# FNet plus MLP-Mixer block in one kernel: first matrix piece loaded from GpSimd, and a smaller idle tile

## The chip, the cores and the metric

The kernel runs on 1 core of one Trainium2 chip. The metric is the device time of one execution in microseconds; the time before is 865.86 us, the median of 3 runs (865.59 to 866.18).

## The reference

With x of 2048 rows and 640 columns (one batch), xn is x with each row brought to mean 0 and variance 1 (eps 1e-5), and the output is a sum of three terms:

```python
xn = layernorm(x)
a, b = xn @ Wd_re.T, xn @ Wd_im.T           # 640 x 640 matrices
fnet = Ws_re @ a - Ws_im @ b                # 2048 x 2048 matrices
h = layernorm(xn)
u = gelu(h.T @ w1 + b1)                     # w1: 2048 x 1728
mixer = (u @ w2 + b2).T                     # w2: 1728 x 2048
out = x + fnet + mixer
```

Everything is float32.

## The kernel before, in words

Each float32 matrix product is made of three TensorE matmuls over operands split into a high and a low part (high by high, high by low, low by high); a *piece* is 128 x 512 values of a matrix that was loaded from memory and is cut into such a pair, the high part by ScalarE (`high`, L143) and the low part by VectorE (`low`, L146). The work is a list of steps; each has a top (cut the high part), a bottom (cut the low part) and a run (its matmuls). The first stage multiplies columns of the sequence matrices, `dft_seq`, with the normalized rows of x (matmuls on L494 and L654); then come the hidden matrices, the two mixer products (`sup`, `sdown`, L154 to L157) and the sums with the output. Program order is the order on each engine, with no reordering (`manual_schedule`).

The start, which the change touches, is written out by hand as a table of words, `START` (L42 to L48). A letter names a function in `first_columns` (table on L556), the number its argument. `x0` to `x7` load 128 rows of x each (320 KB; x0 in two halves of 160 KB, L518; the others on L520). `b0` to `b7` load a piece of `dft_seq` each (256 KB, `load`, L482), and `W1-1-0` and its like load pieces for the next columns (L584). All these loads are issued on SyncE's queue (SP), in the order of the table. Then come the words of the computation: `M` and `A` are the row statistics (L218, L221), `R` the reciprocal root on ScalarE (`near`, L227), `D0` the first block of the high part of row block 0, columns 0 to 255 (`first_hi`, L381, VectorE), `T` and `B` the top and bottom of a step, `O` and `V` the exact factors, five small operations of GpSimd in a chain (L238, L243, L244, L245, L238), `N` and `H` the normalized rows and their high parts on ScalarE (L273) or VectorE (L552), `L` their low parts on VectorE (L146), and `P` a step's matmuls. `T0` cuts piece b0 in two halves: columns 0 to 255 by ScalarE (L143), 256 to 511 by VectorE (CAST, L193). The first real matmul needs both halves and `D0`. Its third pass (`P0-2`) needs the low part of row block 0, which comes at the end of the chain of exact factors.

Ahead of all that, VectorE sets a tile of ones and then a 128 x 512 bfloat16 tile of zeros, `idle` (L137), and TensorE runs ten matmuls of it with itself into a bank that is not read (L140, `WARM`); GpSimd sets `eps` (L133) and runs one operation on it (L135).

Of the kernel before, what the change touches and what calls it, by code (L numbers as in the profile page):

```python
# [10 lines left out]
BF16 = mybir.dt.bfloat16  # L11
AF = mybir.ActivationFunctionType
ALU = mybir.AluOpType

P = 128
# [10 lines left out]
CH = 512  # L26
NC = S // CH
H2 = D // 2
EPS = 1e-5
# [10 lines left out]


START = """  # L42
    x0 b0 W1-1-0 x1 b1 x2 W1-1-1 b2 W1-1-2 x3 b3 W1-1-3 x4 b4 x5 b5 x6 b6 x7 b7 W2-1-0 W2-1-1 W2-1-2 W2-1-3
    M0 A0 R0 D0 T0 O0 V0 H0 B0 T1 P0-0-1 B1 M1 A1 N0 R1 O1 V1 T2 H1 L0 P1-0-1 P0-2 P1-2 B2 M2 A2 T3 R2 O2 T4 V2 H2 B3 N1 P2-0-1 L1 P3-0-1 P2-2 P3-2
    M3 A3 R3 O3 V3 B4 N2 M4 A4 T5 R4 H3 V4 B5 L2 T6 N3 M5 A5 B6 P4-0-1 P5-0-1 P4-2 P5-2 T7 R5 V5 L3 N4 B7 H4 M6 A6 T8 P6-0-1 P6-2 R6 V6 M7 A7 B8 E0-0 E0-1 E0-2 N5 P7
    R7 V7 L4 T9 P8-0-1 P8-2 H5 B9 N6 T10 P9-0-1 L5 P9-2 H6 B10 N7 T11 P10-0-1 L6 P10-2 H7 B11 T12 P11-0-1 L7 P11-2
# [24 lines left out]
def fnet_plus_mixer(  # L71
# [30 lines left out]
    nc = tc.nc  # L102

    keep = ctx.enter_context(tc.tile_pool(name="keep", bufs=1))
# [7 lines left out]
    eps = keep.tile([P, 1], F32, name="eps")  # L112
    idea = keep.tile([P, 1], F32, name="idea")
# [15 lines left out]
    y_part = [[dram.tile([P, ND, CH], F32, name=f"y{m}{c}") for c in range(NC)] for m in range(2)]  # L129


    nc.vector.memset(one, 1.0)
    nc.gpsimd.memset(eps, EPS)  # L133
    nc.scalar.activation(one, one, AF.Abs_reciprocal_sqrt)
    nc.gpsimd.tensor_scalar(idea, eps, EPS, eps, op0=ALU.add, op1=ALU.mult)  # L135
    idle = keep.tile([P, CH], BF16, name="idle", tag="slab7")
    nc.vector.memset(idle, 0.0)  # L137
    psum = [acc.tile([P, CH], F32, name=f"psum{i}") for i in range(8)]
    for i in range(WARM):
        nc.tensor.matmul(psum[7], idle[:, :P], idle, start=True, stop=True)  # L140

    def high(hi, src):
        nc.scalar.activation(hi, src, AF.Copy)  # L143
# [31 lines left out]
    def cut_piece(source, n, tail=False, stacked=False, by_two=False):  # L175

        held = {}

        def of_tail():
            hi, src = (t.rearrange("p (q c) -> p q c", c=P) for t in (held["piece"][:, 0, :n], source()))
            return hi[:, :, :TAIL], hi[:, :, P - TAIL :], src[:, :, :TAIL]

        def top():
            cut_turn[0] = (cut_turn[0] + 1) % (AHEAD + 1)
            held["piece"] = keep.tile([P, 2, D], R32, name="piece", tag=f"cut{cut_turn[0]}")
            if tail:
                hi, _, src = of_tail()
                high(hi, src)  # L190
            elif by_two:
                high(held["piece"][:, 0, : n // 2], source()[:, : n // 2])
                nc.vector.tensor_copy(held["piece"][:, 0, n // 2 : n], source()[:, n // 2 :])  # L193
            else:
                high(held["piece"][:, 0, :n], source())

        def bottom():
            if tail:
                hi, lo, src = of_tail()
                low(lo, src, hi)  # L200
                return held["piece"][:, 0, :n], None
            hi, lo = (held["piece"][:, i, :n] for i in range(2))
            if stacked:
                last = slice(n - P, n)
                low(hi[TAIL:, last], source()[TAIL:, last], hi[TAIL:, last])
            whole = n - P if stacked else n
            low(lo[:, :whole], source()[:, :whole], hi[:, :whole])
            return hi, lo

        return top, bottom  # L210
# [12 lines left out]
    def root(var, q=None):  # L223

        if q is None:
            q = small.tile([P, NS], F32, name="q")[:, : var.shape[-1]]
        nc.scalar.activation(q, var, AF.Abs_reciprocal_sqrt, bias=eps)  # L227
        return var, q

    def inverse(to, var, q):  # L230

        r = small.tile([P, NS], F32, name="r")[:, : var.shape[-1]]
        nc.vector.scalar_tensor_tensor(r, var, EPS, q, op0=ALU.add, op1=ALU.mult)
        nc.vector.scalar_tensor_tensor(r, r, -0.5, q, op0=ALU.mult, op1=ALU.mult)
        nc.vector.scalar_tensor_tensor(to, r, 1.5, q, op0=ALU.add, op1=ALU.mult)
# [12 lines left out]
    def offset(to, ks):  # L248
        nc.vector.scalar_tensor_tensor(to[:, 1, ks], mv[:, ks, 0], -1.0, to[:, 0, ks], op0=ALU.mult, op1=ALU.mult)
# [56 lines left out]
    def fifth(a, which, i):  # L306
        return a[:, which, 7 * Q + i * P : 7 * Q + (i + 1) * P]
# [90 lines left out]
    def later_row(k):  # L398
        return later_pair(k % 4)[:, (k - 8) // 4, :]
# [58 lines left out]
    def c_tile():  # L458

        i = c_turn[0] = (c_turn[0] + 1) % 6  # L460
        return c_place[i // 3][:, i % 3, :]
# [9 lines left out]
    def first_columns():  # L471


        raw = pieces[0].rearrange("p a q c -> p (a q) c")
        banks = {0: psum[0], 1: psum[1], 2: psum[7]}
        vq = {}

        def place_of(i):
            return raw[:, (i + 4) % 8, :]

        def load(i):
            nc.sync.dma_start(place_of(i), dft_seq[0, i])  # L482

        def products(i):
            a, n = fixed[0][i % 4], i // 4

            def run(w, passes=()):
                blocks = [
                    (banks[e], *((a[:, k, n * Q + e * P : n * Q + (e + 1) * P]) for k in range(2))) for e in range(2)
                ] + [(banks[2], fifth(a, 0, n), fifth(a, 1, n))]  # L490
                for one in ([blocks] if passes else [[b] for b in blocks]):
                    for k in passes or range(3):
                        for to, hi, lo in one:
                            nc.tensor.matmul(  # L494
                                to, (hi, hi, lo)[k], w[k % 2], start=k == 0 and i == 0, stop=k == 2 and i % 4 == 3,
                                skip_group_check=True,
                            )
            return run

        def read(i, e):  # L500


            c = c_tile()
            nc.scalar.activation(c, banks[e], AF.Copy)
            if i == 0:
                to = ((1, 4),) if e == 2 else ((1, e), (0, 2 + e), (1, 2 + e))
            else:
                to = ((0, 4 if e == 2 else e),)
            for m, j in to:
                nc.sync.dma_start(y_part[m][0][:, j, :], c)  # L510

        raw_steps.extend(cut_piece(lambda i=i: place_of(i), CH, by_two=i == 0) + (products(i),) for i in range(8))


        def row(k):
            if k == 0:
                for i in range(2):
                    nc.sync.dma_start(x_in[0][:, i * H2 : (i + 1) * H2], x_rows[0][:, i * H2 : (i + 1) * H2])  # L518
            else:
                nc.sync.dma_start(x_in[k], x_rows[k])  # L520

        def begin_loads(i):
            for f in loads.pop(i, ()):
                f()

        def top(i):
            steps[i][0]()

        def bottom(i):
            ready[i] = steps[i][1]()  # L530

        def run(i, *passes):
            steps[i][2](ready[i], *([passes] if passes else []))
            if not passes or 2 in passes:
                del ready[i]

        def rooted(k, to=None, by=1):
            ks = slice(k, (to or k) + 1, by)
            vq[k] = root(mv[:, ks, 1], near[:, 0, ks])

        def inverted(k, to=None, by=1):
            inverse(norm[:, 0, slice(k, (to or k) + 1, by)], *vq[k])

        def factored(k, to=None, by=1):
            inverted(k, to, by)
            offset(norm, slice(k, (to or k) + 1, by))

        def whole_row(k):
            if k in BY_SCALAR:
                return normalize(k, x_in[k], norm)  # L550

            nc.vector.tensor_scalar(  # L552
                x_in[k], x_in[k], mv[:, k, 0:1], norm[:, 0, k : k + 1], op0=ALU.subtract, op1=ALU.mult
            )

        return {  # L556
            "x": row, "b": load, "q": begin_loads, "T": top, "B": bottom, "P": run,
            "M": lambda k: statistics(k, x_in[k] if k < 8 else later_row(k)), "A": aggregate,
            "R": rooted, "F": factored, "I": inverted, "O": lambda k: offset_beside(near, k), "V": factors_beside,
            "D": lambda k: first_hi(),  # L560
            "H": lambda k: first_rows(k, 0), "N": whole_row,
            "L": lambda k: first_rows(k, 1), "E": read,
            "X": lambda i: [f() for f in extras.pop(i)],
            "J": lambda q, j: (sums_left.remove((j, q)), first_sums[q][j]()),
            "W": lambda i, m, q: first_loads.pop((f"B{i}{m}", q))(),
        }
# [580 lines left out]
    start = first_columns()  # L1147
# [49 lines left out]
    gets_hid, _, rests_hid = zip(*(hidden_rows(q, ("x0", "v")[q % 2]) for q in range(3)))  # L1197
# [100 lines left out]
```

## Time and profile before

| | |
|---|---|
| time, median of 3 runs | 865.86 us (865.59 to 866.18) |
| profiled execution, its own time | 865.11 us |
| profiled execution, span from first to last instruction | 863.3 us |
| TensorE busy with matmuls | 858.4 us (99% of the span) |
| VectorE, ScalarE, GpSimd busy | 697.0, 529.2, 179.6 us |
| DMA, mean over the span | 185 GB/s |
| granted TensorE clock, mean | 1.000 |

The span lies 1.8 us below the execution's own time; what is outside it is not in the trace. A row of the chain of waits is a start, a duration and what ran, or which transfer was waited for; a row of the timeline adds the engine, line, operation, tiles and count, and in brackets how long the engine had been idle and what ended that. "SPq" is SyncE issuing transfers, "PEld" a weight load.

### The profile page before, as it was taken

To read this page: it belongs to the slowest core of one execution; us is meant where nothing else is said; L and a number is where in the kernel's file an instruction comes from. 1 tells how busy PE (TensorE), PEld (TensorE's weight loads), DVE (VectorE), ACT (ScalarE), POOL (GpSimd) and SP (SyncE) were. 2 spreads that over 40 slices of the span, in tenths; PEclk is the share of its full clock that TensorE was granted. 3 is DMA by queue.
4 is the path that set the end of the run, shared out by engine and by line. 5 is a ranking of instruction groups with operands and counts; after the bars stand their busy time and mean duration, and the time that the engine had idled before them with its cause. 6 is when DMAs were issued, how large, how long until landed. Compare 5 with 4: busy or idle time off the path is not lost.

```text
span 863.3 us, 13976 instructions
## 1 busy us (share of the span) xinstructions
PE 858.4 (99%) x4882; PEld 786.8 (91%) x4882; DVE 697.0 (81%) x1173; ACT 529.2 (61%) x987; POOL 179.6 (21%) x249
## 2 busy tenths in 40 slices
PE   9999999999999999999999999999999999999998
PEld 6888888888888888889999999999999999999998
DVE  7998868784757888877887788888678978897887
ACT  7766676755444555657565556676577856555654
POOL 5333222212120211122100101111321321101211
PEclk9999999999999999999999999999999999999999
DMA  8879594979593746779576766664678789766776
GB/s 316 287 217 324 127 301 125 253 188 296 145 261 63 200 96 140 175 130 206 114 180 169 158 144 184 195 180 154 149 175 186 160 226 237 184 140 132 155 168 148
DMA packets 93350, 159.44 MB, mean 185 GB/s; under 512 B 9408, under 2 KB 37824, under 8 KB 92928
## 3 DMA queue, kind: packets, MB, share of 16 engines
q0 software_dynamic: 26432, 60.40, 38.4%
q1 hardware_dynamic: 66704, 98.06, 35.0%
q8 instruction: 38, 0.62, 0.3%
q14 instruction: 32, 0.26, 0.1%
q10 hardware_dynamic: 144, 0.08, 0.0%
HBM read 102.05 MB, written 61.70 MB: 190 GB/s over the span
## 4 chain that ended last, share of the span: by engine, by line
PE 99%; DMA 0%; SPq 0%; ACT 0%; DVE 0%; issue 0%; DVEq 0%
PE psum L654 44%; PE psum L155 18%; PE psum L154 18%; PE psum L157 17%; PE psum L494 2%; DMA pieces<-in_dft_seq 0%; SPq L518 0%; ACT piece L143 0%; DVE pair L955 0%; DVEq L1294 0%
## 5 line engine op out<-in xcount | busy, mean ns | idle before, releaser
L146 DVE TENSOR_TENSOR piece<-pieces,piece 128x512 fp32r<-128x512 f32 (+4 forms) x514 | 338.7, 660 | 137.2 <-ACT piece L143 132.1
L143 ACT ACTIVATE piece<-pieces 128x512 fp32r<-128x512 f32 (+3 forms) x490 | 306.6, 626 | 229.7 <-PE psum L654 96.8
L654 PE MATMUL psum<-piece,n 128*128 128x512 f32 x1656 | 377.0, 389 | 0.0
L654 PEld LDWEIGHTS psum<-piece,n 128*128 128x128 f32 x1656 | 310.4, 188 | 65.3 <-DVE piece L146 0.4
L154 PE MATMUL psum<-sup,piece 128*128 128x320 f32 x392 | 120.8, 309 | 0.0
L154 PE MATMUL psum<-sdown,piece 128*128 128x320 f32 x392 | 120.8, 309 | 0.0
L155 PE MATMUL psum<-sdown,piece 128*128 128x320 f32 x392 | 120.8, 309 | 0.0
L155 PE MATMUL psum<-sup,piece 128*128 128x320 f32 x392 | 120.8, 309 | 0.0
L149 DVE TENSOR_TENSOR pieces<-pieces 128x512 f32<-128x512 f32 (+3 forms) x146 | 116.6, 803 | 3.0
L467 POOL DMA_DIRECT2D y<-c x76 | 65.5, 899 | 251.1 <-DVE c L690 132.4
L157 PE MATMUL psum<-sup,piece 128*128 128x320 f32 x368 | 113.7, 309 | 0.0
L157 PE MATMUL psum<-sdown,piece 128*128 128x320 f32 x368 | 113.7, 309 | 0.0
L155 PE MATMUL psum<-shid,piece 128*128 128x320 f32 x280 | 86.5, 309 | 0.0
L154 PE MATMUL psum<-shid,piece 128*128 128x320 f32 x280 | 86.5, 309 | 0.0
L157 PE MATMUL psum<-shid,piece 128*128 128x320 f32 x280 | 86.5, 309 | 0.0
L154 PEld LDWEIGHTS psum<-sup,piece 128*128 128x128 f32 x392 | 73.6, 188 | 0.0
L155 PEld LDWEIGHTS psum<-sdown,piece 128*128 128x128 f32 x392 | 73.6, 188 | 0.0
L154 PEld LDWEIGHTS psum<-sdown,piece 128*128 128x128 f32 x392 | 73.6, 188 | 0.0
L155 PEld LDWEIGHTS psum<-sup,piece 128*128 128x128 f32 x392 | 73.6, 188 | 0.0
L1035 POOL DMA_DIRECT2D out<-pair x38 | 33.0, 950 | 188.9 <-DVE pair L950 161.7
L963 ACT ACTIVATE pair<-psum 128x320 f32<-128x320 f32 x101 | 44.0, 436 | 43.7 <-PE psum L157 40.5
L157 PEld LDWEIGHTS psum<-sup,piece 128*128 128x128 f32 x368 | 69.1, 188 | 0.0
(121 smaller groups left out, 864.3 us busy)
## 6 DMA issues: line engine op xcount, KB each, us to landing
pieces<-in_dft_seq SPq DMA_DIRECT2D x136, 256.0 KB, 5.6
y<-c POOLq DMA_DIRECT2D x106, 256.0 KB, 6.6
pieces<-in_w SPq DMA_DIRECT2D x88, 256.0 KB, 3.9
out<-pair POOLq DMA_DIRECT2D x38, 320.0 KB, 5.7
pieces<-y SPq DMA_DIRECT2D x32, 320.0 KB, 4.2
pieces<-in_w SPq DMA_DIRECT2D x32, 192.0 KB, 3.3
up<-pair POOLq DMA_DIRECT2D x8, 640.0 KB, 3.3
pair<-in_x SPq DMA_DIRECT2D x12, 320.0 KB, 4.5
```

Of the source, the lines that this page charges most:

```text
L143: nc.scalar.activation(hi, src, AF.Copy)
L146: nc.vector.tensor_sub(lo, src, hi.bitcast(F32))
L149: nc.vector.tensor_sub(to, a, b)
L154: nc.tensor.matmul(psum, wh, mh, start=first, stop=False, skip_group_check=True)
L155: nc.tensor.matmul(psum, wh, ml, start=False, stop=last and wl is None, skip_group_check=True)
L157: nc.tensor.matmul(psum, wl, mh, start=False, stop=last, skip_group_check=True)
L467: nc.gpsimd.dma_start(y_part[m][c][:, j, :], t, accum_op=ALU.add)
L494: nc.tensor.matmul(to, (hi, hi, lo)[k], w[k % 2], start=k == 0 and i == 0, stop=k == 2 and i % 4 == 3, skip_group_check=True,)
L654: nc.tensor.matmul(to, (hi, hi, lo)[k], w[k % 2], start=k == 0 and begin, stop=k == 2 and q == 3, skip_group_check=True,)
L963: nc.scalar.activation(c, b, AF.Copy)
L1035: nc.gpsimd.dma_start(out_rows[ts[i]], c[:, i, :], accum_op=ALU.add)
```

## The change

1. `b0` stands first in the table and is issued on GpSimd's queue instead of SyncE's; it is the first instruction of the program there. The other loads stay on SyncE's queue in their order.
2. The two operations on `eps` move behind it on GpSimd (a new word `Z0`, function `constants`).
3. The idle tile shrinks from 512 to 128 columns, is set ahead of the tile of ones, and the idle matmuls read it four times over (a step of 0), still 512 columns each.

```diff
--- before.py
+++ after.py
@@ -40,7 +40,7 @@
 
 
 START = """
-    x0 b0 W1-1-0 x1 b1 x2 W1-1-1 b2 W1-1-2 x3 b3 W1-1-3 x4 b4 x5 b5 x6 b6 x7 b7 W2-1-0 W2-1-1 W2-1-2 W2-1-3
+    b0 x0 Z0 W1-1-0 x1 b1 x2 W1-1-1 b2 W1-1-2 x3 b3 W1-1-3 x4 b4 x5 b5 x6 b6 x7 b7 W2-1-0 W2-1-1 W2-1-2 W2-1-3
     M0 A0 R0 D0 T0 O0 V0 H0 B0 T1 P0-0-1 B1 M1 A1 N0 R1 O1 V1 T2 H1 L0 P1-0-1 P0-2 P1-2 B2 M2 A2 T3 R2 O2 T4 V2 H2 B3 N1 P2-0-1 L1 P3-0-1 P2-2 P3-2
     M3 A3 R3 O3 V3 B4 N2 M4 A4 T5 R4 H3 V4 B5 L2 T6 N3 M5 A5 B6 P4-0-1 P5-0-1 P4-2 P5-2 T7 R5 V5 L3 N4 B7 H4 M6 A6 T8 P6-0-1 P6-2 R6 V6 M7 A7 B8 E0-0 E0-1 E0-2 N5 P7
     R7 V7 L4 T9 P8-0-1 P8-2 H5 B9 N6 T10 P9-0-1 L5 P9-2 H6 B10 N7 T11 P10-0-1 L6 P10-2 H7 B11 T12 P11-0-1 L7 P11-2
@@ -129,15 +129,13 @@
     y_part = [[dram.tile([P, ND, CH], F32, name=f"y{m}{c}") for c in range(NC)] for m in range(2)]
 
 
+    idle = keep.tile([P, P], BF16, name="idle", tag="slab7")
+    nc.vector.memset(idle, 0.0)
     nc.vector.memset(one, 1.0)
-    nc.gpsimd.memset(eps, EPS)
     nc.scalar.activation(one, one, AF.Abs_reciprocal_sqrt)
-    nc.gpsimd.tensor_scalar(idea, eps, EPS, eps, op0=ALU.add, op1=ALU.mult)
-    idle = keep.tile([P, CH], BF16, name="idle", tag="slab7")
-    nc.vector.memset(idle, 0.0)
     psum = [acc.tile([P, CH], F32, name=f"psum{i}") for i in range(8)]
     for i in range(WARM):
-        nc.tensor.matmul(psum[7], idle[:, :P], idle, start=True, stop=True)
+        nc.tensor.matmul(psum[7], idle, idle[:, None, :].to_broadcast([P, CH // P, P]), start=True, stop=True)
 
     def high(hi, src):
         nc.scalar.activation(hi, src, AF.Copy)
@@ -479,7 +477,7 @@
             return raw[:, (i + 4) % 8, :]
 
         def load(i):
-            nc.sync.dma_start(place_of(i), dft_seq[0, i])
+            (nc.sync if i else nc.gpsimd).dma_start(place_of(i), dft_seq[0, i])
 
         def products(i):
             a, n = fixed[0][i % 4], i // 4
@@ -519,6 +517,10 @@
             else:
                 nc.sync.dma_start(x_in[k], x_rows[k])
 
+        def constants(_):
+            nc.gpsimd.memset(eps, EPS)
+            nc.gpsimd.tensor_scalar(idea, eps, EPS, eps, op0=ALU.add, op1=ALU.mult)
+
         def begin_loads(i):
             for f in loads.pop(i, ()):
                 f()
@@ -554,7 +556,7 @@
             )
 
         return {
-            "x": row, "b": load, "q": begin_loads, "T": top, "B": bottom, "P": run,
+            "x": row, "b": load, "Z": constants, "q": begin_loads, "T": top, "B": bottom, "P": run,
             "M": lambda k: statistics(k, x_in[k] if k < 8 else later_row(k)), "A": aggregate,
             "R": rooted, "F": factored, "I": inverted, "O": lambda k: offset_beside(near, k), "V": factors_beside,
             "D": lambda k: first_hi(),
```

On SyncE, at the start of the program, the queue before holds x0 (two halves), b0, the first piece of the next columns, x1 and b1 (`pieces_120` on L482 is first b0, then b1):

```order
L518 DMA x_75<-in_x 128x320 x2
L482 DMA pieces_120<-in_dft_seq 128x512
L584 DMA pieces_121<-in_dft_seq 128x512
L520 DMA x_75<-in_x 128x640
L482 DMA pieces_120<-in_dft_seq 128x512
```

and after the change the row of b0 is gone, and the same loads stand one place earlier:

```order
L516 DMA x_75<-in_x 128x320 x2
L586 DMA pieces_119<-in_dft_seq 128x512
L518 DMA x_75<-in_x 128x640
L480 DMA pieces_118<-in_dft_seq 128x512
L518 DMA x_75<-in_x 128x640
```

So x0 is still the first thing that SyncE issues, and the loads behind it move up by one issue; the last two rows are b1 and x2.

On GpSimd, the rows before, from the branch into the program to the first operation that works on row block 0:

```order
L1294 UNCONDITIONAL_BRANCH
L133 MEMSET eps 128x1
L135 ISA
L135 TENSOR_SCALAR idea<-eps 128x1
L238 TENSOR_SCALAR near<-mv,near 128x1
```

and after:

```order
L1296 UNCONDITIONAL_BRANCH
L480 DMA pieces_118<-in_dft_seq 128x512
L521 MEMSET eps 128x1
L522 ISA
L522 TENSOR_SCALAR idea<-eps 128x1
L236 TENSOR_SCALAR near<-mv,near 128x1
```

The load of b0 (`pieces_118`) went in ahead of the constants; nothing else moved on GpSimd.

## Rows read from the trace of the kernel before

**Rows 1.** The page, part 1: busy time, share of span, instructions.

```profile
PE 858.4 (99%) x4882; PEld 786.8 (91%) x4882; DVE 697.0 (81%) x1173; ACT 529.2 (61%) x987; POOL 179.6 (21%) x249
```

**Rows 2.** Chain of waits, 0 to 12 us: start, duration in us, what.

```profile
0.76 0.39 SPq L518
...
1.21 0.41 SPq L518
...
1.66 3.83 DMA pieces<-in_dft_seq
...
5.51 0.42 ACT piece L143
...
5.98 2.12 PE psum L494 x6
8.10 1.38 PE psum L654 x6
```

**Rows 3.** Timeline, TensorE's matmuls and weight loads.

```profile
1.24 4.45 PE L140 MATMUL psum<-idle 128*128 128x512 bf16 x10 [1.24 <-DVE idle L137]
...
2.07 0.15 PEld L140 LDWEIGHTS <-idle 128*128 128x128 bf16 x1 [0.27 <-issue]
...
2.49 0.15 PEld L140 LDWEIGHTS <-idle 128*128 128x128 bf16 x1 [0.28 <-issue]
...
9.16 0.59 PEld L494 LDWEIGHTS psum<-piece,n 128*128 128x128 f32 x3
...
9.32 0.86 PE L494 MATMUL psum<-piece,n 128*128 128x512 f32 x3
...
31.37 367.47 PE L654 MATMUL psum<-piece,n 128*128 128x512 f32 x1620
```

**Rows 4.** Tile x, 0 to 6 us: durations in ns, first and last start.

```profile
L218 DVE BATCH_NORM_STATS2 st<-x x2: 494/494/495, 3.0 to 3.6; 128x6 f32<-128x320 f32 x2
```

**Rows 5.** Timeline, VectorE, 0 to 10 us.

```profile
0.91 0.27 DVE L137 MEMSET idle<- 128x256 uint32 x1
...
4.12 0.21 DVE L221 BATCH_NORM_AGGREGATE mv<-st 128x2 f32<-128x12 f32 x1
4.75 0.41 DVE L381 TENSOR_SCALAR n<-x,mv,near 128x256 fp32r<-128x256 f32 x1 [0.43 <-ACT near L227]
5.51 0.29 DVE L193 CAST piece<-pieces 128x256 fp32r<-128x256 f32 x1 [0.35 <-DMA pieces<-in_dft_seq]
...
8.68 0.62 DVE L146 TENSOR_TENSOR n<-x,n 128x256 fp32r<-128x256 f32 x2
```

**Rows 6.** Timeline, ScalarE, 0 to 10 us.

```profile
4.42 0.29 ACT L227 ACTIVATE near<-mv,eps 128x1 f32<-128x1 f32 x1 [2.18 <-DVE mv L221]
5.51 0.42 ACT L143 ACTIVATE piece<-pieces 128x256 fp32r<-128x256 f32 x1 [0.79 <-DMA pieces<-in_dft_seq]
...
7.73 0.92 ACT L273 ACTIVATE x<-x,norm 128x640 f32<-128x640 f32 x1 [0.89 <-POOL norm L238]
...
9.48 0.99 ACT L273 ACTIVATE n<-x,near 128x256 fp32r<-128x256 f32 x2
```

**Rows 7.** Timeline, GpSimd, 0 to 10 us.

```profile
0.75 0.10 POOL L133 MEMSET eps<- 128x1 f32 x1 [0.29 <-POOLq L1287]
...
4.82 0.40 POOL L238 TENSOR_SCALAR near<-mv,near 128x1 f32<-128x1 f32 x1 [3.59 <-ACT near L227]
...
6.88 0.81 POOL L238 TENSOR_SCALAR norm<-mv,norm 128x1 f32<-128x1 f32 x1
```

**Rows 8.** Stretches (us): busy us and count by engine, clock, DMA share, GB/s.

```profile
1.75:2.00 0.25, 0.25 (x2) 0.04 (x1) 0.00 (x0) 0.25 (x1) 0.00 (x0) 1.00 0.75 159
2.00:3.00 1.00, 1.00 (x4) 0.38 (x3) 0.00 (x0) 0.23 (x2) 0.00 (x0) 1.00 1.00 291
3.00:3.50 0.50, 0.50 (x3) 0.22 (x2) 0.45 (x1) 0.00 (x0) 0.00 (x0) 1.00 0.96 141
...
9.30:12.00 2.70, 2.70 (x13) 2.25 (x13) 2.49 (x7) 2.41 (x6) 2.30 (x6) 1.00 1.05 408
```

**Rows 9.** Timeline, GpSimd's first DMA.

```profile
35.58 1.30 POOL L465 DMA_DIRECT2D y<-c  x2 [7.77 <-ACT c L678]
```

**Rows 10.** DMA queues from 35.58 to 36.88 us: packets, MB, share of 16 engines.

```profile
q1 hardware_dynamic: 232, 0.41, 82.2%
```

**Rows 11.** DMA queues from 36.88 to 37.08 us, the same columns.

```profile
q0 software_dynamic: 19, 0.08, 99.6%
q1 hardware_dynamic: 5, 0.01, 13.1%
```

## The prediction

> **What bounds the kernel now.** The page's busy times come first: TensorE is busy for 858.4 of 863.3 us [rows 1], so the whole program is one stream of matmuls, and only two things can move the end: when the stream begins, and holes in it. From 31.37 us on, 1620 matmuls take 367.47 us, 0.227 us each, the pace of 512 columns at 2.4 GHz with a little over [rows 3]; nothing there waits, and nothing that was lost at the start can be made good. So the second view is the chain of waits over the first 12 us [rows 2]. It shows three issues on SyncE, two for x0 (0.76 and 1.21 us) and one for b0 (1.66 us), then 3.83 us until b0 has landed at 5.49, then ScalarE's 0.42 us for b0's half, and the first real matmul at 5.98. By this view b0's transfer is what the start waits for.
>
> The chain shows only the wait that ended last. The third view, the timelines, shows the others. x0's halves have landed when their statistics start, at 3.05 and about 3.6 us [rows 4]. From the second half on: statistics to 4.08, aggregate to 4.33, the block of the high part from 4.75 to 5.16 on VectorE [rows 5], with the root in between on ScalarE, 4.42 to 4.71 [rows 6]. GpSimd's chain of exact factors starts at 4.82 and ends at 6.88 + 0.81 = 7.69 [rows 7]; ScalarE then normalizes x0 until 8.65 [rows 6], VectorE makes its low part from 8.68 [rows 5], and the third pass, whose weight load waits for that, gets it at 9.16; its matmuls run from 9.32 [rows 3]. Before those, TensorE had twelve real matmuls to do, and it finished them at 9.32 as well: x0's chain and b0's chain meet there with at most 0.16 us between them. **This second meeting is what the chain of waits does not show.**
>
> **The change, part by part.** *b0 alone, earlier.* If x0 stayed as it is, b0 would no longer be last at the first matmul. ScalarE would cut its half after the root, from 4.72 to 5.14, and VectorE its half after the block of the high part, from 5.2 to 5.5 (0.29 us [rows 5]). The first matmul would start at about 5.5 instead of 5.98, 0.48 us earlier. But the third pass would still wait for x0's low part until 9.16, so of this at most 9.32 - 9.16 = 0.16 us is left there. I take -0.1 for this part alone, with ends at -0.16 and 0.
>
> *What b0 does to x0.* GpSimd's first operation starts at 0.75 us [rows 7]. The only price for a transfer's start on its queue is its first DMA, far away: issued at 35.58 us [rows 9], no packet of its queue until 36.88 [rows 10], 19 in the next 0.2 us [rows 11]; 1.30 us. So b0's packets would begin near 0.75 + 1.30 = 2.05 us. x0's began at about 1.75, 1 us after its issue (the stretch from there has the first traffic, at 159 GB/s [rows 8]). By 2.05 x0 has moved 0.25 x 159 + 0.05 x 291 KB per us, about 55 KB of its 328 KB, so 273 KB are still to come when b0's 262 KB join. The DMA engines are then busy 1.00 of the time [rows 8]: a byte of b0 is a byte that x0 does not get. If the two queues share the engines evenly, the two transfers end at nearly the same time, and x0's second half is late by nearly all of b0: 262 KB at 408 GB/s, the best rate in the rows, is 0.64 us; at 291 GB/s, the rate while x0 moves alone, 0.90. The lower end is 0: b0 could start too late to meet x0, which has landed by 3.6 [rows 4], or get only what x0 leaves. I take 0.64, because two queues that are both full are nearer to the later stretch than to the first. The Trainium skill, page "DMA: Bandwidth & Descriptors", section "Issuing engines are not separate DMA queues", says that transfers started by different engines run on the same 16 DMA engines and interleave, and that issuing on several engines saves only the issue time. It speaks against this change: by it the shift of x0 is the full share of b0, by a reading of the queues as separate it would be 0.
>
> *The sum.* With x0's second half at about 4.23 instead of 3.59, everything that hangs on it moves by 0.64: the block of the high part ends at 5.80, VectorE's half of b0 at about 6.12, and the first matmul starts at 6.15, 0.17 later than before. The twelve matmuls would be through at 9.49. The exact factors end at 8.33, x0 is normalized at 9.29, and the third pass gets its low part at 9.16 + 0.64 = 9.80. So the third pass starts at 9.80 instead of 9.32: **+0.48 us**. The next meeting, the high part of row block 1 at 9.48 + 0.99 = 10.47 on ScalarE [rows 6], moves to 11.11 by the same chain; TensorE, itself 0.48 late, wants it at 11.18. No more is added, and the pace behind it has no slack in which to win this back.
>
> *SyncE's queue.* It loses one issue, 0.43 us per load behind b0. x0's two issues stand ahead of it and don't move; the later loads start one place earlier, behind the same bytes in total. The 0.5 us in which the engines moved only 141 GB/s [rows 8] may fill up; that helps x1 and b1, which were not waited for. I set 0, ends -0.1 and 0.
>
> *The constants on GpSimd* start after its issue, about 0.7 us later (half of 1.30 for two [rows 9]). ScalarE first wants `eps` at 4.42 [rows 6]; hidden by some 2.5 us of waiting for x0. 0.
>
> *The idle tile.* Its zeros take 0.27 us now [rows 5]; a quarter of the width, and first in line, lets the idle matmuls begin some 0.2 to 0.3 us before 1.24. Each still streams 512 columns; reading 128 four times changes no count. They are not waited for: their end moves from 5.69 to about 5.4, ahead of the first matmul in every case. 0 for the path, but the idle stretch before the first real matmul grows from 0.30 us to about 0.7; that is a rival below.
>
> The sum against the profiled execution is 865.11 + 0.48 = 865.59; that execution lies 0.75 below the median of the runs, so against the median it is 865.86 + 0.48 = 866.34, and I say **866.3 us**. What a measurement of this kernel can tell from no change is about 0.2%, 1.7 us; so this is no change.
>
> **The rivals.** *A: x0 is not held up*: b0's bytes go in gaps. For it: 291 GB/s while x0 moves, and 141 behind it, are below the 408 that the engines reach later [rows 8]. Against: DMA share 1.00 from 2 to 3 us. Then the first part alone counts: -0.1 to -0.2, 865.7.
>
> *B: b0 comes no earlier.* A first DMA on GpSimd could start slower at 0.75 us than at 35.58, and end beside the first piece of the next columns. From a landing at 5.49 or later the old order of events is back: 865.9, up to +0.4 more if it lands up to 0.4 later. For it: one row is all there is for GpSimd's start. Against: it would have to start 1.5 us later than that row says.
>
> *C: the clock rises later; slower.* The idle matmuls follow each other at 2.49 - 2.07 = 0.42 us [rows 3], 512 columns at 1.2 GHz, and the first six real ones take 2.12 us from 5.98, the next six 1.38 [rows 2]: the faster level comes at about 7.0 us, although the granted clock is printed as 1.00 in every stretch [rows 8]. TensorE had then been busy since 1.24 with one hole of 0.30 us. If the longer hole made the chip start over, the level would rise as long after 6.15 as it did after 1.24, 5.8 us, at 12.0. By then 14 matmuls would be done, where the kernel before had done them at about 9.5: +2.5 us, 868.4. It decides from the point where the hole is long enough to count. Against it: a hole of 0.30 did not, and 0.7 is still a small part of what went before. The Trainium skill, "TensorE: Matmul & The Clock Gate", Part 1, has the engine throttled by default and released by activity; the trace agrees in the two paces, 0.42 and 0.23 us. The reverse, a level that rises earlier since the idle matmuls start earlier, would save at most the 0.5 us that the first matmuls lose at the lower pace, and x0's chain would eat most of it.
>
> **How the numbers follow.** The forecast (x0 late, 866.0 to 866.9) has 0.50; A (865.2 to 865.9 with the scatter of the runs, 0.3 to either side) 0.32; B (865.6 to 866.5) 0.11; C 0.05; what I don't see 0.02. Leaving out the tails of A and C gives 865.2 to 867.1. Faster by over 0.2% would need 1.7 us, and the whole time between the earliest possible first matmul, 5.5, and now is 0.5: 0.01. Slower by over 0.2% is C and little else: 0.05. Within 0.2%: 0.94.
>
> **What would show it.** Right: the second statistics of x0 start near 4.2 us, b0's cut no longer waits for its DMA, the first matmul starts at 6.0 to 6.2, and the weight load of the third pass waits for VectorE until about 9.8; the chain of waits goes through x0 in place of b0. Wrong: x0's second statistics still at 3.6 (A), b0's halves still the last to be ready (B), or matmuls 0.43 us apart behind 7.1 us (C). A change of more than 1.7 us with none of these would mean that the end, not the start, has moved.

## The result, and the profile after

The changed kernel takes **866.87 us**, the median of 22 runs (865.38 to 869.16), against 865.31 us (864.89 to 866.18) for the kernel before, measured beside it in as many runs. The ratio is 1.0013, with a 95% interval of 1.0007 to 1.0019: slower by about 1.1 us by the ratio and 1.6 us by the medians. That is inside the 0.2% that the prediction called no change, but it is clear of zero. The spread tells as much as the median: before, all runs lie within 1.3 us; after, within 3.8 us.

The profiled execution took 866.81 us, its span is 864.7 us, 1.4 us more than before. The busy time of TensorE has not changed at all (page, part 1; compare [rows 1]):

```profile
PE 858.4 (99%) x4882; PEld 786.3 (91%) x4882; DVE 697.2 (81%) x1173; ACT 529.2 (61%) x987; POOL 178.8 (21%) x250
```

So the 1.4 us are waiting. The two executions' times differ by more, 1.7 us: what lies outside the span, time less span, is 2.1 us after the change and 1.8 before. That is so in every execution, 2.06 to 2.18 us in the 22 of the change, and the experiments come back to it. Inside the span, the chain of waits over the first 14 us, in the columns of [rows 2], shows where most of the waiting began:

```profile
0.65 0.65 issue
1.30 5.34 DMA pieces<-in_dft_seq
6.64 0.02 issue
6.67 0.42 ACT piece L141
7.09 0.04 issue
7.13 1.69 PE psum L492 x6
8.83 1.36 PE psum L656 x6
10.19 0.88 PE psum L492 x3
```

GpSimd is free for b0's load at 0.65 us and starts it at 1.30; b0 has landed at 6.64, where it had landed at 5.49 before. Nothing of x0 is in this chain. The first real matmul starts at 7.13 instead of 5.98, 1.15 us later. The first six then take 1.69 us instead of 2.12 and win 0.43 of it back, as TensorE ran at its faster level by then.

Tile x, 0 to 6 us, the row that answers to [rows 4], shows that x0 was not touched: its statistics start at the same times as before.

```profile
L216 DVE BATCH_NORM_STATS2 st<-x x2: 494/494/495, 3.1 to 3.6; 128x6 f32<-128x320 f32 x2
```

TensorE's timeline, to be held against [rows 3], gives the sizes:

```profile
1.00 4.45 PE L138 MATMUL psum<-idle 128*128 128x512 bf16 x10 [1.00 <-DVE one L134]
7.13 1.69 PE L492 MATMUL psum<-piece,n 128*128 128x512 f32 x6 [1.68 <-ACT piece L141]
...
10.09 0.97 PE L492 MATMUL psum<-piece,n 128*128 128x512 f32 x3
10.90 0.85 PE L656 MATMUL psum<-piece,n 128*128 128x512 f32 x3
11.59 1.52 PE L492 MATMUL psum<-piece,n 128*128 128x512 f32 x6
```

The idle matmuls begin 0.24 us earlier and end at 5.45; then TensorE has nothing for 1.68 us, where it had 0.30. The third pass starts at 10.09 instead of 9.32 (+0.77). Of this 0.72 is what the first six left over; the rest is a short wait for VectorE, in whose order x0's low part stands behind the cuts of b0 and b1 and the statistics of row block 1, and these came late. Behind it the shift, worked out here and below as the start of the matmul of the same number in both traces, after minus before, is +0.89 (11.59, where the like matmuls started at 10.70 before) and stays between 0.72 and 0.93 until 444 us. The rest came in one piece at 450 us, where the whole of TensorE's waiting behind 12 us is one row (TensorE's waits, whole span: engine, line, what it waited for, us, times, longest):

```profile
PE psum L492 <- ACT piece L141: 1.7, 1, 1.7
PE psum L138 <- DVE one L134: 1.0, 1, 1.0
PE psum L152 <- ACT pair L965: 0.3, 1, 0.3
```

There the shift grows from 0.90 to 1.46 us, with a chain that goes back over VectorE to a load of partial sums from memory. This was no part of the prediction.

### The profile page after: what moved, and what is told of

Same layout as the page of the kernel before. It is cut to its first block, busy times and chain, and to the rows that moved or that the text cites. A ratio compares the mean times of both kernels' runs of the same rounds, so it can differ in the third digit from the quotient of the medians.

```text
span 864.7 us, 13976 instructions
## 1 busy us (share of the span) xinstructions
PE 858.4 (99%) x4882; PEld 786.3 (91%) x4882; DVE 697.2 (81%) x1173; ACT 529.2 (61%) x987; POOL 178.8 (21%) x250
## 4 chain that ended last, share of the span: by engine, by line
PE 97%; DMA 1%; DVE 1%; ACT 0%; issue 0%; DVEq 0%; ACTq 0%; POOLq 0%
PE psum L656 43%; PE psum L152 17%; PE psum L153 17%; PE psum L155 17%; PE psum L492 2%; DMA pieces<-y 1%; DMA pieces<-in_dft_seq 1%; DVE piece L144 0%; DVE pieces L147 0%; ACT piece L141 0%; DVE pieces L877 0%; DVE pair L147 0%; ACT sup L141 0%; DVE sup L144 0%; DVE pair L952 0%
```

## The experiments

Two theories stood against each other at first: theory 1, that b0's late landing over GpSimd is the loss; theory 2, that the longer stretch between the idle and the first real matmuls makes TensorE lose its faster level in some executions. With them went the prediction's own step, x0 held up by b0.

**The idle tile alone.**

```diff
+    idle = keep.tile([P, P], BF16, name="idle", tag="slab7")
+    nc.vector.memset(idle, 0.0)
     nc.vector.memset(one, 1.0)
...
-    idle = keep.tile([P, CH], BF16, name="idle", tag="slab7")
-    nc.vector.memset(idle, 0.0)
...
-        nc.tensor.matmul(psum[7], idle[:, :P], idle, start=True, stop=True)
+        nc.tensor.matmul(psum[7], idle, idle[:, None, :].to_broadcast([P, CH // P, P]), start=True, stop=True)
```

> The kernel before with the idle tile of the change alone; b0 stays third on SyncE's queue. Theory 1 (the loss is b0's late landing over GpSimd, 6.64 us instead of 5.49): no loss, the median within 0.3 us of before, first real matmul at 5.9 to 6.0. Theory 2 (the loss is TensorE's clock, which falls or rises late in the executions where the stretch between the idle matmuls and the first real one is too long): this stretch grows by the 0.23 us that the idle matmuls begin earlier, so a part of the executions is 1 us or more slower and the median is 0.3 us or more above before.

Measured: 865.25 us (865.14 before), ratio 0.9999 (0.9990 to 1.0008). The first real matmul started at 6.22, where 5.9 to 6.0 was expected, as b0 landed later here as well (its cut began at 5.75, in [rows 6] at 5.51). Reading 128 columns four times, and beginning 0.23 us earlier, costs and brings nothing that can be seen. No execution's mean granted clock is below 0.999, so none shows the clock's loss: the 0.23 us alone were too little for that here. The expectation of theory 2, as it stood, failed here.

**b0 on GpSimd alone, idle tile as before.**

```diff
-    x0 b0 W1-1-0 x1
+    b0 x0 Z0 W1-1-0 x1
...
-            nc.sync.dma_start(place_of(i), dft_seq[0, i])
+            (nc.sync if i else nc.gpsimd).dma_start(place_of(i), dft_seq[0, i])
```

> b0 first on GpSimd's queue as in the change, the idle tile as before (512 columns). Theory 1: the same as the change, about 1.5 us above before, b0 landed at about 6.6, first real matmul at about 7.1. Theory 2: the idle matmuls end 0.23 us later, so fewer executions lose the clock; the median lies below the change's by 0.3 to 1 us, with the same two groups of times. If the idle tile is the whole loss: as before.

Measured: 865.93 us (865.14 before), ratio 1.0011 (1.0002 to 1.0019), in two groups: seven runs at 865.5 to 866.0, four at 866.5 to 867.5. So moving b0 brings a loss by itself, of 0.8 us by the medians; the change itself, at 1.6, was not run beside it. That is what theory 2 expected, two groups and a median below the change's. The profiled execution, 867.27 us, is one of the upper group, and it shows theory 2 at work. TensorE's timeline:

```profile
1.24 3.79 PE L138 MATMUL psum<-idle 128*128 128x512 bf16 x10 [1.24 <-DVE idle L135]
6.86 2.35 PE L492 MATMUL psum<-piece,n 128*128 128x512 f32 x6 [1.82 <-ACT piece L141]
9.00 2.50 PE L656 MATMUL psum<-piece,n 128*128 128x512 f32 x6
11.34 0.86 PE L492 MATMUL psum<-piece,n 128*128 128x512 f32 x3
```

and stretches of the same execution, with the columns of [rows 8]:

```profile
4.30:7.60 3.30, 1.48 (x7) 0.62 (x6) 1.51 (x4) 1.51 (x4) 1.51 (x5) 1.00 1.03 385
7.70:11.00 3.30, 3.30 (x9) 2.65 (x9) 2.83 (x8) 2.31 (x6) 0.91 (x3) 0.50 1.05 402
11.10:14.00 2.90, 2.90 (x14) 2.39 (x13) 2.07 (x5) 1.68 (x5) 1.38 (x5) 1.00 1.05 393
```

The granted clock was 1.00 (2.4 GHz) when the real matmuls began; the ten idle ones, in 3.79 us instead of 4.45, had already ended at that pace. Between 7.6 and 7.7 us, 0.8 us behind a stretch in which TensorE had been without work for 1.82 us, it fell to 0.50 (1.2 GHz). It came back at 11 us. Such a stretch does not always do it: the change's own profiled execution has one of 1.68 us and no fall. In 3.3 us only 9 matmuls ran, where 14 ran in the 2.9 us behind them; the third pass starts at 11.34, 1.25 us later than in the profiled execution of the change, although b0 landed 0.27 us earlier (chain: 1.31 + 5.06 = 6.37).

**More idle matmuls.**

```diff
-WARM = 10
+WARM = 14
```

> The change with 14 idle matmuls instead of 10, so that TensorE has work until about 6.5 to 7 us. Theory 1: b0 still lands at about 6.6; the median stays 1.0 to 1.5 us above before. Theory 2: no execution loses the clock, the group of times above 867 is gone, and the median comes down to 0.2 to 0.8 us above before, since only the later start of the first matmuls is left.

Measured: 866.02 us (865.14 before), ratio 1.0008 (1.0000 to 1.0017); all runs between 865.41 and 866.77. The upper group is gone and 0.9 us remain (0.6 in the repetition below), no less than with b0 on GpSimd and 10 idle matmuls beside it. Theory 2 is shown for the upper group; that the rest is theory 1, b0's landing, is not shown by this run: in its profiled execution b0's cut began at 5.65, 0.14 us later than in [rows 2], and the time was 865.41, the fastest of the eleven. The repetition's profiled execution was the fastest of its eleven too, so no trace shows why the span of the middle execution is longer. Over all runs the mean granted clock of a span tells the same: 7 of the change's 22 runs have 0.997 or 0.998, all of them at 867.05 to 867.76 us, as have 2 of the 11 with b0 on GpSimd and 10 idle matmuls; with 14 idle matmuls it is none of 22 (this run and its repetition below), and of 96 runs of the kernel before one. Of the remaining runs of the change some are late with the clock at 1.000, up to 869.16; no trace shows them, and the next run shows that a mean of 1.000 does not rule the clock out.

**b0 on ScalarE's queue.**

```diff
-    nc.scalar.activation(one, one, AF.Abs_reciprocal_sqrt)
...
-            (nc.sync if i else nc.gpsimd).dma_start(place_of(i), dft_seq[0, i])
+            (nc.sync if i else nc.scalar).dma_start(place_of(i), dft_seq[0, i])
...
         def constants(_):
+            nc.scalar.activation(one, one, AF.Abs_reciprocal_sqrt)
             nc.gpsimd.memset(eps, EPS)
```

> The change with b0 as the first instruction of ScalarE's queue instead of GpSimd's (ScalarE's first operation on the tile of ones moves behind it). Both theories: b0 is issued at about 0.75 and its packets begin at about 1.8, beside x0's. If the two queues share the engines as the prediction had it, x0's second half lands at about 4.2 instead of 3.6, the first real matmul starts at about 6.1, and the time is 0.3 to 0.6 us above before. If x0 is not held up, the first matmul starts at about 5.5 and the time is 0.1 to 0.3 below before. Theory 2 expects one group of times, as the stretch without matmuls is under 0.9 us.

Measured: 866.13 us (865.14 before), ratio 1.0011 (1.0002 to 1.0020). Here b0 does start beside x0 (issued at 0.75), and x0 is held up. Tile x, 0 to 7 us, and VectorE's timeline:

```profile
L215 DVE BATCH_NORM_STATS2 st<-x x2: 494/494/494, 4.0 to 4.5; 128x6 f32<-128x320 f32 x2
```
```profile
5.71 0.41 DVE L378 TENSOR_SCALAR n<-x,mv,near 128x256 fp32r<-128x256 f32 x1 [0.43 <-ACT near L224]
6.04 0.28 DVE L190 CAST piece<-pieces 128x256 fp32r<-128x256 f32 x1
```

Both halves of x0 come 0.9 us later than in [rows 4], and b0's cut no longer waits for its transfer: it stands behind x0's block. This is the prediction's step, with 0.9 where it took 0.64; its upper price, b0's bytes at the 291 GB/s of x0's own stretch, was 0.90. TensorE's timeline:

```profile
6.47 2.90 PE L491 MATMUL psum<-piece,n 128*128 128x512 f32 x6 [1.02 <-DVE piece L190]
9.17 1.86 PE L656 MATMUL psum<-piece,n 128*128 128x512 f32 x6
```

The first matmul starts at 6.47, where 6.1 was expected, and the matmuls run at the slower pace, 0.43 us each, up to about 9.8 us. So the third pass starts at 10.86, 1.54 us later than before, although x0's low part was only 0.74 us later (VectorE begins it at 9.42, at 8.68 in [rows 5]). This execution took 866.86 us, one of the two slowest, and its mean granted clock reads 1.000: the column does not show a level that rises late. The median is a little above the 0.3 to 0.6 us that were expected, and how much of its 1.0 us is x0's delay and how much the clock is not shown.

**SyncE's later loads held back.**

```diff
-    b0 x0 Z0 W1-1-0 x1 b1
+    b0 x0 Z0 M0 G0 W1-1-0 x1 b1
...
-    M0 A0 R0 D0
+    A0 R0 D0
...
+            "G": lambda _: nc.vector.memset(pieces[1].rearrange("p a q c -> p (a q) c")[:, :, 0:1], 0.0),
```

with 14 idle matmuls; the written columns are overwritten by the loads.

> The change with 14 idle matmuls, and SyncE's loads behind x0 held back until VectorE has read x0 (it writes one column of each buffer of the next pieces after x0's statistics, and the next load waits for that). So b0's packets share the engines with x0's last ones only, up to about 4.1 us. If b0 lands late because its packets take turns with those of the next loads, it lands at about 4.3 to 4.8 us here, and its cuts start right behind the root at 4.7. If its late landing is GpSimd's queue itself (a late start, or packets that are slow one by one), it lands at 5.5 or later, as in the change. Later loads are late by some 2.5 us, so the time as a whole says nothing and is expected above the change's.

Measured, in one profiled execution: GpSimd's load starts at 1.30 us as in the change, and b0 is ready before ScalarE can take it. ScalarE's timeline:

```profile
4.36 0.29 ACT L225 ACTIVATE near<-mv,eps 128x1 f32<-128x1 f32 x1 [2.11 <-DVE mv L219]
4.77 0.42 ACT L141 ACTIVATE piece<-pieces 128x256 fp32r<-128x256 f32 x1
5.18 0.49 ACT L271 ACTIVATE n<-x,near 128x128 fp32r<-128x128 f32 x1
```

The transfers' queues from 4.5 to 7 us (packets, MB, share of 16 engines), first of the change, where a quarter of b0 is still on its way, then here, where the row of GpSimd's queue, q0, is absent:

```profile
q1 hardware_dynamic: 417, 0.85, 94.2%
q0 software_dynamic: 33, 0.07, 7.9%
```
```profile
q1 hardware_dynamic: 279, 0.59, 72.3%
```

So b0's late landing in the change's profile is not GpSimd's start alone. With a start at 1.30 it lands before 4.8 us with SyncE's next loads held back, and at 6.64 if SyncE's next loads run beside it. Before, b0 stood ahead of those loads in one queue; on a queue of its own it shares with them. The time, 867.08 us, tells nothing, as the held loads were late.

**The constants first on GpSimd.**

```diff
-    b0 x0 Z0 W1-1-0 x1 b1
+    Z0 b0 x0 W1-1-0 x1 b1
```

with 14 idle matmuls.

> The change with 14 idle matmuls, and the two operations on eps ahead of b0's load on GpSimd. In the change the load started at 1.30 although the engine was free at 0.65 us. If that 0.65 us is a price of the load on this queue, it starts at about 1.25 + 0.65 = 1.9 us and b0 lands about 0.6 us later than in the change. If it is a start-up that runs out anyway at about 1.3 us, the load starts at 1.3 to 1.4 and nothing else moves.

Measured, GpSimd's timeline of one profiled execution:

```profile
0.97 0.26 POOL L522 TENSOR_SCALAR idea<-eps 128x1 f32<-128x1 f32 x1
1.46 0.72 POOL L480 DMA_DIRECT2D pieces<-in_dft_seq  x1 [0.23 <-issue]
```

The load starts at 1.46, 0.16 us later than with nothing ahead of it: near the second outcome (1.3 to 1.4). Most of the 0.65 us runs out by itself and can be filled with other work. b0's cut began at 6.49, and the time was 866.42 us.

**Before, with 14 idle matmuls.**

```diff
-WARM = 10
+WARM = 14
```

> The kernel before with 14 idle matmuls instead of 10. Theory 2 (clock): no execution loses the clock at the start, and the first real matmuls run at the faster level more often; the time is 0 to 0.4 us below before, and the rare executions near 867 are gone. Without theory 2: no change, or up to 0.5 us slower if the idle matmuls run past 5.98.

Measured: 865.38 us (865.45 before), ratio 1.0000 (0.9991 to 1.0009), all runs from 864.89 to 865.87, before from 864.90 to 866.60. The spread is smaller, the median the same. In the profiled execution (865.74 us) b0's cut began at 6.40, 0.89 us later than in [rows 2], though nothing had changed for b0: it lands at different times on SyncE's queue too. By its chain of waits the idle matmuls then ran until 7.09, and the first real matmul came right behind them.

**x0 on two queues.**

```diff
-                    nc.sync.dma_start(x_in[0][:, i * H2
+                    (nc.scalar if i else nc.sync).dma_start(x_in[0][:, i * H2
```

with 14 idle matmuls, and ScalarE's first operation on the tile of ones behind that load.

> The kernel before with 14 idle matmuls, and x0's second half as the first instruction of ScalarE's queue; b0 stays on SyncE's queue, now its second load. x0 as a whole lands 0.2 to 0.3 us earlier, as its second half no longer waits for SyncE's second issue; b0 is issued 0.43 us earlier and lands 0.2 to 0.4 us earlier. Both chains that meet at the third pass move together, so the time is 0.2 to 0.5 us below before. If the start of x0's second half beside the first only slows the first, x0's statistics end at the same time and only the clock is gained.

Measured: 865.38 us (865.45 before), ratio 0.9999 (0.9990 to 1.0008). Not as expected: the two halves, both issued near 0.75, landed 2.8 and 3.0 us later, and their statistics started at 3.56 and 3.97 instead of 3.05 and 3.59. So the first half came 0.5 us later and the second, at about 3.7, no earlier than before. b0 came early, and the gain and the loss met at the third pass, at 9.31 (9.32 before).

**One late copy on GpSimd.** This and the last two runs look at the second loss, at 450 us. Transfers are counted on eight semaphores per kind of queue, in turn; one load that changes queues shifts the turn of every later one on both.

```diff
-            loads[COPIES_AT[t]].append(lambda t=t, of=of: nc.sync.dma_start(out_rows[t][of], x_rows[t][of]))
+            loads[COPIES_AT[t]].append(lambda t=t, of=of, i=i: (nc.sync if t or i else nc.gpsimd).dma_start(out_rows[t][of], x_rows[t][of]))
```

> The kernel before with one late, unhurried transfer moved from SyncE's queue to GpSimd's: the first of the copies of x rows into the output, at about 100 us. From there on both queues count their transfers as in the change (SyncE one fewer, GpSimd one more), while the start is that of before. If the change's second loss, the stop of TensorE by 0.56 us at 450 us, comes from that shift of the counting, a stop of 0.1 to 0.6 us is seen near 450 us and the median is 0.1 to 0.6 us above before. If not, no such stop, and the median is within 0.1 us of before.

Measured: 865.82 us (865.11 before), ratio 1.0010 (1.0001 to 1.0019). The time moved the way that was expected of the shift, by 0.7 us where 0.1 to 0.6 was expected, but the profiled execution (865.88 us) has no stop at 450 us: its shift there grows from 0.49 to 0.55 us only. Its 0.49 arose at the start, where the two kernels are the same, by a b0 that landed at 6.19 over SyncE's queue. So the run says nothing on the stop.

It does settle another 0.3 us. Time less span is 2.08 to 2.18 us in all its executions, and 1.77 to 1.90 in those of the kernel before beside it, though b0 is on SyncE's queue in both. Over all runs here, with spans kept to 0.1 us, it is 2.05 to 2.19 us in each of the 68 executions of a kernel with one transfer more on GpSimd's queue (this run, the change and its variants with b0 there, but for the one below that restores the count), and 1.72 to 1.92 in each of the 162 of the others, b0 on ScalarE's queue among them. So about 0.3 us of the change's loss is no wait at the start at all: it lies outside the span and comes with the one transfer more on GpSimd's queue, whichever it is. What happens there the trace does not show.

**A version meant to beat both.**

```diff
-WARM = 14
+WARM = 11
...
+        by = nc.gpsimd if k else nc.vector
-        nc.gpsimd.tensor_scalar(r, mv[:, k, 1:2], EPS, q, op0=ALU.add, op1=ALU.mult)
+        by.tensor_scalar(r, mv[:, k, 1:2], EPS, q, op0=ALU.add, op1=ALU.mult)
```

and the same in the three operations that follow; the rest as with x0 on two queues.

> A version meant to beat both: the kernel of the run with x0 on two queues, with 11 idle matmuls, and the exact factors of row block 0 on VectorE, between its cut of b0 and b0's low part, instead of GpSimd. If the third pass waits for x0's chain by way of GpSimd, as the prediction had it, its low part comes 0.7 us or more earlier, the third pass no longer waits, and the first matmul at about 5.8 is what counts: 0.2 to 0.4 us below before. If the second meeting (row block 1 on ScalarE) is no earlier, the gain is lost there, and the time is within 0.1 us of before.

Measured: 865.21 us (865.11 before), ratio 1.0003 (0.9994 to 1.0012). TensorE's timeline:

```profile
5.96 0.94 PE L494 MATMUL psum<-piece,n 128*128 128x512 f32 x3 [0.39 <-DVE beside L243]
7.33 0.96 PE L494 MATMUL psum<-piece,n 128*128 128x512 f32 x3 [0.44 <-DVE piece L145]
8.13 1.52 PE L654 MATMUL psum<-piece,n 128*128 128x512 f32 x6
9.49 0.84 PE L494 MATMUL psum<-piece,n 128*128 128x512 f32 x3
```

The third pass no longer waits for its low part, but the second does: the exact factors now stand ahead of b0's low part on VectorE, and the matmuls wait 0.44 us for that. Nothing is gained. No version here beats the kernel before.

**The counting restored.**

```diff
-            nc.gpsimd.dma_start(later_pair(q)[:, i, :], x_rows[8 + q + 4 * i])
+            (nc.sync if (q, i) == (0, 1) else nc.gpsimd).dma_start(later_pair(q)[:, i, :], x_rows[8 + q + 4 * i])
```

in the change with 14 idle matmuls, beside that kernel without it:

> The change with 14 idle matmuls, and one later transfer (the second load of the later rows of x, at about 38 us) moved from GpSimd's queue to SyncE's, so that from there on both queues have issued as many transfers as before the change. If the shift of the counting costs time late in the program (the stop at 450 us in the change, the 0.7 us of the run with one copy on GpSimd), the median is 0.3 to 0.7 us below that of the same kernel without this move. If the late start of the first matmul is all that is left, both are the same, 0.7 to 1.0 us above before.

> The change with 14 idle matmuls once more, beside the run with the restored counting and on the same chip, as its measure: 0.7 to 1.0 us above before, all executions below 867.

Measured: 865.66 us restored, 865.99 us not, 865.40 us before; ratios to before 1.0001 (0.9992 to 1.0010) and 1.0002 (0.9993 to 1.0011). The repetition came 0.6 us above before and once at 867.02, where 0.7 to 1.0 and nothing above 867 was expected. The ranges of the two (865.32 to 866.58 and 865.49 to 867.02) overlap nearly wholly, and the kernel before had six of its 21 runs at 866.7 to 867.4 here. But the 0.33 us between the two medians are what lies outside the span: 1.74 to 1.86 us in all eleven executions with the count restored, 2.05 to 2.19 in all eleven without, while the medians of the spans are 863.9 and 863.8. So restoring the count takes the 0.3 us away, with b0 still first on GpSimd's queue.

Neither profiled execution stops at 450 us, though the counting of the second is that of the change. The run with SyncE's loads held back stops there as the change does (shift from 1.05 to 1.63 us), and with the constants first it grows from 0.75 to 0.99. So the stop is not in every execution, and its cause stays open.

## Why the prediction was right, and where it was wrong

**The number.** 866.3 us was forecast, 865.2 to 867.1, and 866.87 came; slower, by less than 0.2%. The sum of +0.48 us was too small: the medians say +1.6, the ratio +1.1. The 865.86 that it was added to, a median of three, lies 0.55 above the 865.31 measured beside the change, which hid a third of the difference. And the time came by another way than the forecast's: by the prediction's own signs, x0's second statistics at 3.6 and b0's halves the last to be ready were marks of its being wrong. That the time fell into the range is in good part luck.

**What bounds the start.** Right: TensorE's busy time did not move, and what was late at the third pass, which the prediction named as the second meeting (+0.77), was not won back.

**b0's start: the step that failed.** "b0's packets would begin near 0.75 + 1.30 = 2.05 us." The load started at 1.30, not 0.75, and GpSimd's queue had moved no packet by 2.88 us and one by 2.95; 1.6 us from issue to packet, where [rows 9, 10] had 1.30. By then nearly all of x0 was through: SyncE's queue had moved 0.31 MB, and x0 is 0.33. So x0's second half "late by nearly all of b0", by 0.64 us, did not happen, and with it fell the forecast's chain of x0. The two rows had priced a queue in the middle of the program; at its start it was slower by 0.55 us before the issue and 0.3 behind it.

**What b0 does to x0.** Right as a mechanism, shown where the step before it was made true: on ScalarE's queue b0 starts with x0, x0 is 0.9 us late, and the time is 1.0 us above before, though in the profiled execution a level that rose late is part of that. The Trainium skill, page "DMA: Bandwidth & Descriptors", section "Issuing engines are not separate DMA queues", says that transfers of different issuers share the engines; the trace agrees, with 0.9 us here. In the change itself the roles were reversed: b0 was the one that was held up, by SyncE's next loads. The run with those loads held back shows it: ready before 4.8 us instead of 6.64.

**Rival B** had the right event for the profiled execution, b0 no earlier, and the wrong size: "up to +0.4 more" was a first matmul 1.15 us later. It looked at when b0 would start and not at what would be beside it then. Before, the next loads came behind b0 in one queue. Loads that move up "behind the same bytes in total", costed at nothing, were what ran beside b0. But one profile of each kernel makes too much of this: with the same loads, b0's cut began at 5.51, 5.75, 6.21 and 6.40 over SyncE's queue (before, the idle tile alone, the late copy, before with 14) and at 5.65, 5.74, 5.88, 6.39 and 6.67 over GpSimd's (14 idle matmuls, counting restored, the repetition, GpSimd alone, the change). The means are 5.97 and 6.07. That b0's lateness made this one execution slow is shown; that b0 is later on average over GpSimd's queue is not, and nothing here says that it is earlier, which the forecast's chain needed. Of what is left of the loss with 14 idle matmuls, 0.6 to 0.9 us by medians, 0.3 lies outside the span. The other 0.3 to 0.6 stays open between a scatter of landings that is a little worse and the late stop.

**Rival C**, the clock, with a chance of 0.05, happened in about a third of the change's runs by their mean clock, in a milder form. The priced form was a level that rises late, +2.5 us; a level that rises late was seen with b0 on ScalarE's queue, about 0.8 us of the third pass's 1.54 there (1.54 less the 0.74 of x0's low part). With b0 on GpSimd's queue, seen was a level that had risen and fell again behind 1.82 us without work, worth about 1.5 us (from the first real matmul to the third pass 4.48 us, 2.96 in the change's profiled execution). The prediction took the idle stretch to be 0.7 us; with b0 late it was 1.7 to 1.8. With 14 idle matmuls no execution of the change took longer than 867.02 us, where 10 of the 22 had. By the medians 0.9 and 0.6 us are left of 1.6, but the change was not run beside these, so the difference prices the clock only roughly.

**Costed at nothing.** The idle tile and the constants: right, by the run with the idle tile alone and by GpSimd's chain, which began its factors at 4.80 (4.82 before). The sum took what lies outside the span as unchanged; it grew by 0.3 us, with the number of transfers on GpSimd's queue. Half a microsecond at 450 us in the profiled execution was not foreseen and is not explained.

## What to carry to other kernels

A transfer that moves to a queue of its own shares the engines with all that the other queue issues meanwhile, and the place that it had ahead of those loads is gone, so before a transfer is moved to another queue, look at what will run beside it, and not only at when it is issued. The price of a queue's first transfer should not be taken from a row in the middle of the program. Idle matmuls that are to hold the clock should last until the first real one: a fixed number of them is tuned to one landing time, and a later landing can cost twice, by itself and by the clock. And compare time less span before and after: part of a loss may lie outside the trace.

## What the runs showed of the hardware

- GpSimd's first load started 0.65 us after the engine was free, and with two small operations ahead of it at 1.46 instead of 1.30: most of the delay runs beside other work.
- b0's landing varies by up to 0.9 us between profiled executions on one queue (5.51 to 6.40 for the start of its cut over SyncE's), as much as the change seemed to cost. And the time follows the landing only in part: 6.40 came with 865.74 us, 6.21 with 865.88, 5.51 with 865.11. Matmuls that start later may already run at the faster level: with 6.40 the first real one was 0.89 us later than before, and the third pass 0.51. A difference of half a microsecond at the start needs more than one profile of each kernel.
- The granted clock is printed as 1.00 ahead of the first change that is recorded, also where matmuls of 512 columns follow each other at 0.43 us. In such a stretch the pace tells the level, and the column doesn't.
- One transfer more on GpSimd's queue, whichever it was, made the time outside the span 0.3 us longer in every execution (2.05 to 2.19 us against 1.72 to 1.92). One fewer on SyncE's queue, with b0 on ScalarE's instead, did not (1.78 to 1.90).
